# Decode attention: turning K in place on VectorE, and QK with a block-diagonal q

## The chip, the cores and the metric

One core of a Trainium2 chip. The metric is the device time of one execution in microseconds (us), lower is better. The experiments ran in five groups, each with the kernel before beside them and on another chip (0, 3, 14, 15 and 12 in the record); its medians agree within 0.2 us (384.60 to 384.79), so times are compared across groups. A ratio is the mean time of one kernel's fast runs over that of the kernel before in the same rounds, with a 95% interval, so it is not quite the ratio of the medians quoted beside it. The span in a profile is some 2 us shorter than the device time.

## The reference, cut to what matters

One decoding step of a transformer layer for a batch of 4: layer norm, attention over a sliding window of 4096 cached keys, and a gated MLP.

```python
B, Sq, D = 4, 1, 576
Hq, Hkv, Sk, Dh = 32, 16, 16384, 128
W = min(4096, max(256, Sk // 4))                       # 4096
q = (x @ wq) ...                                        # 32 heads of 128
k = jnp.repeat(k_cache[:, :, Sk - W:, :], rep, axis=1)  # rep = 2
v = jnp.repeat(v_cache[:, :, Sk - W:, :], rep, axis=1)
p = softmax(einsum("bhqd,bhkd->bhqk", q, k) * Dh ** -0.5)
o = einsum("bhqk,bhkd->bhqd", p, v) ... @ wo
h = x + attention(layernorm(x))
out = h + (relu(n @ W_gate) * (n @ W_up)) @ W_down      # n = layernorm(h)
```

K and V of the window are 67 MB each in bf16, the weights some 25 MB: 160 MB that have to come from HBM, for little arithmetic.

With these inputs the attention is only about 5e-5 in an output of about 0.05 (a float32 emulation off the chip gave standard deviations of 4.9e-5 and 0.049). **The comparison with the reference therefore hardly sees errors of the attention.**

## The kernel before

K and V each come in 16 tiles of 4 MB (one batch, four KV heads, all 4096 keys). A partition holds a block of 128 keys of one head: partition = 4 x (key block) + head. Four slots of SBUF form a ring, and all loads stand in one queue in program order: K0, wq (which takes one slot of the ring), K1, K2, K3, K4, V0, K5, V1, K6, V2 and so on. A load is issued when the last reader of its slot is done.

```python
def add_kv(kind, g):
    b, qd = divmod(g, 4)
    s = ring_slot()
    off = slot0 + s * TILE
    src = cache[b, 4*qd:4*qd+4, SK-WIN:SK, :].rearrange("a (p t) d -> p a (t d)", p=32)
    place((kind, g), off, TILE, ("TR", 4*g+3) if kind == "K" else ("PV", 4*g+3),   # who frees the slot
          lambda e: e.dma_start(out=arena[:, off:off+TILE], in_=src), key=f"slot{s}")
...
def pe_tr(i):            # TensorE turns K: 2048 transposes of 128x128 into PSUM
    ... e.transpose(out=bankb[TRB[j]][:, u*128:(u+1)*128], in_=kn[:, t, :], identity=perm)
def evac(i, j):          # VectorE and ScalarE take turns to bring it back to SBUF
    ... (dve e.tensor_copy | act e.copy)(out=kT[...], in_=bankb[TRB[j]])
def pe_qk(dd):           # q of one head against K, in four column groups side by side
    ... e.matmul(bank[4+w][32*j:32*j+32, :], lhsT=qTm[:, b, 4*qd+a, :], rhs=k[:, j, :, a, :], ...)
```

A K slot is free as soon as its transposes are done. The turned K lies in a buffer of its own, and q is needed only there.

## Time and profile before

384.78 us (median of 4, 384.63 to 384.81).

| engine | busy us | share |
|---|---|---|
| TensorE (PE) | 248.7 | 65% |
| VectorE (DVE) | 159.0 | 42% |
| ScalarE (ACT) | 146.4 | 38% |
| input DMA queue (q1) | | 97.4% of 16 engines |

From the profile's page of the kernel before: busy time by engine, two rows of the 40 slices (of 9.6 us each; digits are tenths), the DMA queues, the engines' shares of the chain that ended last, and the groups of instructions for turning K and for QK (busy us, mean ns of one, idle time before them).

```profile
PE 248.7 (65%) x3781; PEld 185.9 (49%) x3781; DVE 159.0 (42%) x277; ACT 146.4 (38%) x162; POOL 8.7 (2%) x36
DMA  8999999999999999999999999999999999999992
GB/s 329 439 433 432 410 421 437 434 433 433 425 423 433 427 433 435 427 420 433 437 430 435 424 428 427 427 428 439 437 432 415 421 436 451 416 431 426 416 411 113
...
q1 hardware_dynamic: 6352, 159.59, 97.4%
q8 instruction: 29, 0.48, 0.5%
...
DMA 69%; PE 27%; DVE 2%; SPq 1%; ACT 1%; issue 0%
...
L425 PE MATMUL psb<-sb_perm,sb_arena 128*128 128x128 bf16 x2048 | 140.3, 235 | 74.0 <-DMA sb_arena<-in_A_k_cache_dram 73.8
L441 ACT COPY sb_arena<-psb 128x1024 bf16<-128x1024 bf16 x128 | 123.0, 1021 | 141.1 <-PE psb L425 141.1
L439 DVE COPY sb_arena<-psb 128x1024 bf16<-128x1024 bf16 x128 | 87.0, 689 | 112.1 <-PE psb L425 111.6
L457 PE MATMUL psb<-sb_arena,sb_qTm 128*32 128x512 bf16 x512 | 38.0, 423 | 0.9 <-DVE sb_qTm L404 0.9
```

Read the GB/s row first: it never dips between the first slice and the last. The kernel is bound by its 160 MB at about 430 GB/s. Every engine has idle time and most of it (the last column) waits for DMA, or for an engine that does.

### The profile page before, as it was taken

Reading aid. Unit: us, or ns where it says so; the run is one execution under the profiler, and the core shown is the slowest. Engines: PE = TensorE matmul, PEld = TensorE weight load, DVE = VectorE, ACT = ScalarE, POOL = GpSimd, SP = SyncE. Lnnn points to the kernel's source line nnn. Section 1 sums busy time; section 2 is a strip of 40 time slices with the busy share of each in tenths; the row PEclk is TensorE's granted clock in tenths of the full one; section 3 lists DMA queues with packets and bytes.
Section 4 is the critical chain, followed back from the end, with each engine's and each line's share of the span. In section 5 each row is a group of like instructions: output and inputs, shape, how many; then the busy total and the mean of one; then the engine's idle time right before and its main releaser. Section 6 shows DMA issues by size and latency. Waiting matters only on the chain.

```text
span 382.6 us, 8170 instructions
## 1 busy us (share of the span) xinstructions
PE 248.7 (65%) x3781; PEld 185.9 (49%) x3781; DVE 159.0 (42%) x277; ACT 146.4 (38%) x162; POOL 8.7 (2%) x36
## 2 busy tenths in 40 slices
PE   0664999779492938893947667966759366026753
PEld 0643788557371726672726455745546222003532
DVE  3342565665342434774432426752516454002220
ACT  3341688836161524762433428542525401000010
POOL 7100000000000000000000000000000000000000
PEclk9997999999888796999796969996969657555597
DMA  8999999999999999999999999999999999999992
GB/s 329 439 433 432 410 421 437 434 433 433 425 423 433 427 433 435 427 420 433 437 430 435 424 428 427 427 428 439 437 432 415 421 436 451 416 431 426 416 411 113
DMA packets 6408, 160.09 MB, mean 418 GB/s; under 512 B 740, under 2 KB 744, under 8 KB 1384
## 3 DMA queue, kind: packets, MB, share of 16 engines
q1 hardware_dynamic: 6352, 159.59, 97.4%
q8 instruction: 29, 0.48, 0.5%
q14 instruction: 3, 0.02, 0.0%
q10 hardware_dynamic: 24, 0.01, 0.0%
HBM read 159.58 MB, written 0.00 MB: 417 GB/s over the span
## 4 chain that ended last, share of the span: by engine, by line
DMA 69%; PE 27%; DVE 2%; SPq 1%; ACT 1%; issue 0%
DMA sb_arena<-in_A_k_cache_dram 53%; PE psb L425 18%; DMA sb_arena<-in_B_W_down_dram 8%; DMA sb_arena<-in_A_v_cache_dram 8%; PE psb L457 5%; PE psb L505 2%; PE psb L480 1%; DVE sb_pp L487 1%; ACT sb_pp L468 1%; SPq L280 0%; DVE sb_stat L464 0%; DVE sb_o_sel L516 0%; PE psb L539 0%; PE psb L530 0%; DVE sb_o_tmp L512 0%
## 5 line engine op out<-in xcount | busy, mean ns | idle before, releaser
L425 PE MATMUL psb<-sb_perm,sb_arena 128*128 128x128 bf16 x2048 | 140.3, 235 | 74.0 <-DMA sb_arena<-in_A_k_cache_dram 73.8
L441 ACT COPY sb_arena<-psb 128x1024 bf16<-128x1024 bf16 x128 | 123.0, 1021 | 141.1 <-PE psb L425 141.1
L425 PEld LDWEIGHTS psb<-sb_perm,sb_arena 128*128 128x128 bf16 x2048 | 131.5, 106 | 89.3 <-DMA sb_arena<-in_A_k_cache_dram 79.8
L439 DVE COPY sb_arena<-psb 128x1024 bf16<-128x1024 bf16 x128 | 87.0, 689 | 112.1 <-PE psb L425 111.6
L505 PE MATMUL psb<-sb_arena,sb_pp 128*32 128x512 bf16 x512 | 35.9, 425 | 19.9 <-DMA sb_arena<-in_A_v_cache_dram 19.9
L457 PE MATMUL psb<-sb_arena,sb_qTm 128*32 128x512 bf16 x512 | 38.0, 423 | 0.9 <-DVE sb_qTm L404 0.9
L505 PEld LDWEIGHTS psb<-sb_arena,sb_pp 128*32 128x32 bf16 x512 | 12.9, 104 | 36.3 <-DMA sb_arena<-in_A_v_cache_dram 20.9
L512 DVE TENSOR_TENSOR sb_o_tmp<-psb,sb_qm 128x512 f32<-128x512 f32 x16 | 11.1, 692 | 41.2 <-PE psb L505 41.2
L487 DVE TENSOR_TENSOR sb_pp<-psb,sb_am 128x1024 bf16<-128x1024 bf16 x16 | 19.6, 1223 | 16.2 <-PE psb L480 16.2
L480 PE MATMUL psb<-sb_ident_b,sb_pp 128*128 128x128 bf16 x128 | 11.5, 242 | 15.8 <-DVE sb_pp L487 8.3
L468 ACT ACTIVATE sb_pp<-psb,sb_stat 128x2048 bf16<-128x2048 f32 x8 | 15.8, 1975 | 9.7 <-DVE sb_stat L466 9.7
L457 PEld LDWEIGHTS psb<-sb_arena,sb_qTm 128*32 128x32 bf16 x512 | 11.6, 103 | 14.8 <-issue 6.2
L480 PEld LDWEIGHTS psb<-sb_ident_b,sb_pp 128*128 128x128 bf16 x128 | 8.6, 108 | 18.8 <-ACT sb_pp L468 8.1
L516 DVE TENSOR_REDUCE sb_o_sel<-sb_o_tmp 128x128 f32<-128x512 f32 x16 | 16.4, 1024 | 0.5
L612 ACT COPY sb_pp<-psb 128x288 f32<-128x288 f32 x1 | 0.4, 399 | 36.2 <-PE psb L607 36.2
L654 PE MATMUL psb<-sb_arena,sb_hnT 128*32 128x384 bf16 x120 | 7.5, 421 | 4.1 <-DVE sb_hnT L639 2.2
L654 PEld LDWEIGHTS psb<-sb_arena,sb_hnT 128*32 128x32 bf16 x120 | 4.1, 121 | 7.2 <-DMA sb_arena<-in_B_W_up_dram 2.3
L464 DVE TENSOR_REDUCE sb_stat<-psb 128x1 f32<-128x1024 f32 x4 | 4.9, 1221 | 4.6 <-PE psb L457 4.6
L687 PE MATMUL psb<-sb_arena,sb_pp 128*32 128x144 bf16 x144 | 3.7, 251 | 4.1 <-DMA sb_arena<-in_B_W_down_dram 3.6
L534 ACT ACTIVATE sb_stat<-sb_stat 128x1 f32<-128x1 f32 x4 | 0.9, 213 | 13.1 <-DVE sb_stat L532 13.1
L661 DVE TENSOR_TENSOR sb_pp<-psb,sb_pp 128x384 bf16<-128x384 f32 x3 | 1.5, 551 | 9.6 <-PE psb L654 9.6
L687 PEld LDWEIGHTS psb<-sb_arena,sb_pp 128*32 128x32 bf16 x144 | 2.6, 105 | 5.1 <-DMA sb_arena<-in_B_W_down_dram 4.6
(128 smaller groups left out, 78.7 us busy)
## 6 DMA issues: line engine op xcount, KB each, us to landing
sb_arena<-in_A_k_cache_dram SPq DMA_DIRECT2D x16, 4096.0 KB, 28.3
sb_arena<-in_A_v_cache_dram SPq DMA_DIRECT2D x16, 4096.0 KB, 33.6
sb_arena<-in_A_wo_dram SPq DMA_DIRECT2D x1, 4608.0 KB, 20.7
sb_arena<-in_B_W_gate_dram SPq DMA_DIRECT2D x1, 4608.0 KB, 34.1
sb_arena<-in_B_W_up_dram SPq DMA_DIRECT2D x1, 4608.0 KB, 43.5
sb_arena<-in_A_wq_dram SPq DMA_DIRECT2D x1, 4096.0 KB, 23.0
sb_arena<-in_B_W_down_dram SPq DMA_DIRECT2D x3, 1296.0 KB, 30.0
sb_arena<-in_B_W_down_dram SPq DMA_DIRECT2D x1, 864.0 KB, 31.6
```

The source lines that it names most:

```text
L425: o = pe(("TRJ", i, j), lambda e, j=j, u=u, t=t: e.transpose(out=bankb[TRB[j]][:, u * 128:(u + 1) * 128], in_=kn[:, t, :], identity=perm[: ...
L439: dve(("EV", i, j), lambda e: e.tensor_copy(out=dst, in_=src), deps)
L441: act(("EV", i, j), lambda e: e.copy(out=dst, in_=src), deps)
L457: o = pe(("QK", dd), lambda e, a=a, j=j: e.matmul(bank[4 + w][32 * j:32 * j + 32, :], lhsT=qTm[:, b, 4 * qd + a, :], rhs=k[:, j, :, a, :], ...
L468: act(("EXP", b, w), lambda e: e.activation(out=p_sb[:, 2048 * w:2048 * w + 2048].rearrange("p (k a) -> p k a", a=4), in_=bass.AP(tensor=p ...
L480: pe(("PT", b, r), lambda e, tl=tl: e.transpose(out=mb_ps[:, tl * 128:(tl + 1) * 128], in_=p_sb[:, (r * 8 + tl) * 128:(r * 8 + tl + 1) * 128],
L487: dve(("PM", b, r), lambda e: e.tensor_tensor(out=dst, in0=src, in1=msk, op=ALU.mult), [("PT", b, r), "c_am8", ("PV", 16 * b - 1) if b els ...
L505: pe(("PV", i), lambda e, j=j, lo=lo, pm=pm, tb=tb: e.matmul(o_ps[32 * j:32 * j + 32, :], lhsT=pT[:, pm:pm + 32], rhs=v[:, lo:lo + 512], s ...
L512: dve(("OS", g), lambda e: e.tensor_tensor(out=o_tmp[:, :].rearrange("p (t d) -> p t d", t=4), in0=o_ps.rearrange("p (t d) -> p t d", t=4) ...
L516: dve(("OSEL", g), lambda e: e.tensor_reduce(out=o_sel[:, qd, :], in_=o_tmp[:, :].rearrange("p (t d) -> p d t", t=4), axis=AX.X, op=ALU.ad ...
L654: pe(("GU", g, c // 4), lambda e, g=g, m=m, j=j, lo=lo, c=c: e.matmul(bank[3 * g + m][32 * j:32 * j + 32, 0:384], lhsT=hnT[:, c if c < 4 e ...
L687: pe("DOWN", lambda e, j=j, r=r, n=n, wv=wv: e.matmul(bank[0][32 * n:32 * n + 32, 0:144], lhsT=hhT[:, r * 128 + 32 * j:r * 128 + 32 * j + 32],
```

## The change

Its intent: take the turning of K from TensorE, and the copies out of PSUM from VectorE and ScalarE. VectorE turns each half tile by one transpose of 128x4096 four-byte elements (pairs of bf16), in place; the layout takes it that this works in blocks of 32x32 (no trace shows the blocks). Since a pair of bf16 stays together, QK has to take the even and odd elements of d in separate matmuls; since the blocks are taken to stay in their 32 partitions, q is laid out block-diagonally over four groups of 32 partitions. The heads lie as partition mod 4, and the transpose writes them two by two: each 16 bytes of a partition of the turned K hold (head 0, key 0), (head 1, key 0), (head 0, key 1), (head 1, key 1), or the same of heads 2 and 3.

```diff
-            place((kind, g), off, TILE, ("TR", 4 * g + 3) if kind == "K" else ("PV", 4 * g + 3),
+            place((kind, g), off, TILE, ("QK", g, 1) if kind == "K" else ("PV", g),
...
-        def pe_tr(i): ... 2048 transposes on TensorE
-        def evac(i, j): ... 256 copies out of PSUM
+        def turn_k(g, w):
+            k = arena[:, land[("K", g)] + w * QWW:][:, 0:QWW].bitcast(FP32)
+            dst = k.rearrange("p (n h l a) -> p n l h a", h=2, l=2, a=2)
+            src = k.rearrange("p (n l h a) -> p n l h a", h=2, l=2, a=2)
+            dve(("TRA", g, w), lambda e: e.transpose(out=dst, in_=src), ...)
...
+        def pe_qk(g, w):
+            for a in range(4):            # head
+                for cb in range(4):       # half of d, even or odd
+                    off = land[("K", g)] + w * QWW + cb // 2 * 64 + a // 2 * 8 + a % 2 * 2 + cb % 2
+                    wo_ = b % 2 * QWW + (4 * qd + a) * 512 + cb * 128
+                    e.matmul(bank[SB[b % 2] + w], lhsT=arena[:, wo_:wo_ + 128],
+                        rhs=bass.AP(tensor=arena, offset=off, ap=[[AW, 128], [128, 64], [16, 4], [4, 2]]), ...)
```

(cuts marked with ...; P is turned on VectorE in the same way, its heads masked by the bias of the exponential; the tail is unchanged.) A K slot is now freed by QK, which needs q, and no longer by the transposes. And the pattern [4, 2] at the end of rhs says that a QK matmul finds exactly two elements in each 16 bytes of a partition, 8 bytes apart. (The texts call such 16 bytes a line.)

## The prediction

> **What bounds the kernel now.** DMA. The page gives 97.4% as the input queue's share of 16 engines, and every slice between the first and the last reads 9. In 4 us windows no stretch before 372 us is empty, whether PE is busy or idle (426 GB/s at 120-124 us with PE at zero). 160 MB over 2.5 to 379 us is 425 GB/s. In the chain of waits, 69% is DMA; its 18% of PE transposes are only what happened to be followed back through buffer releases while other transfers were queued. PE (65%), VectorE (42%) and ScalarE (38%) all have slack. So work taken from them is worth nothing unless it shortens the start (2.5 us) or the tail (3.3 us after the last landing), and neither is touched.
>
> **What the change removes.** 2048 PE transposes (140 us busy), their evictions on ScalarE (123 us) and VectorE (87 us), the P transposes (11.5) and masked copies (19.6).
>
> **What it adds.**
> - VectorE: 32 transposes of 4096 four-byte elements. The trace gives 1.04 ns per element (128x512 from PSUM 0.69 us, 128x1024 reduction 1.22), so about 4.4 us each, 8.8 a K tile, 140 in all. [...] Eight P transposes of 2048, 2.2 us each. VectorE ends near 210 us (55%).
> - PE: QK as 512 full-width matmuls of 512 columns instead of four side by side. Four took 0.245 us warm, 0.45 cold, so one should take 0.22 to 0.43: 7 to 10 us a tile, 115 to 150 us in all, against 178 for transposes plus QK before. [...]
> - ScalarE: 32 exponentials of 512 and 16 small q copies, near 30 us.
>
> **Critical path.** Steady state: one K and one V tile take 19.6 us of DMA. VectorE needs 8.8 + 1.7 (select) + about 1.6 (softmax share) = 12; PE 9 to 13. A K slot is freed about 15 us after landing (transpose 4.4, select 1.7, transpose 4.4, QK 3.5 to 5) instead of about 12; three other slots cover 29 us. No stall.
> Start: K slot 0 is now freed by QK, which needs q, not by the transposes. wq lands at 25-26 us; projection, q transposes and copies give q near 31-33 us; QK of tile 0 ends near 39-42. The queue still holds K2 until about 45 us, so K3 is issued with 1 to 4 us in hand. This is the tightest place; it could cost 0 to 3 us. The 8192-element memset on GpSimd (about 7 us from 0.84 ns per element) is ready near 10 us, before q.
> Tail: P of the last batch is ready about 27 us after K15 lands, as before (308 against 281 us), and after V15 all is as before.
>
> **Prediction.** 385.3 us, 8 in 10 between 382.5 and 391. Faster by over 2%: 0.02; within 2%: 0.87; slower: 0.11.
>
> **What would show it.** DMA tenths stay 9, GB/s near 425. VectorE transposes near 4.4 us and VectorE busy near 210. PE busy drops to 160-220, ScalarE below 50. Chain even more DMA. If the start step is wrong: a window below 300 GB/s at 38-50 us.
>
> **What would make it wrong.** If the four-byte transpose runs at half rate (8.7 us), VectorE needs about 20.5 us per pair, above DMA's 19.6: the last K is turned some 40 us late and the time rises 5% or more. If two-per-line reads slow QK twofold and the clock stays low, PE reaches 17 to 30 us a pair, similar. [...]

Three sentences are cut from it, where marked: two quoted rules, and one named a risk. The 4.4 us a transpose come from 1.04 ns per element and the 0.22 to 0.43 us a matmul from four side by side (0.245 and 0.45 us), both in the trace of the kernel before, and the forecast stays 385.3 us, 0.5 above the 384.78 before. That QK's read of two elements per 16 bytes costs nothing extra was the assumption; no trace had shown it.

## More of the kernel before

Times are of runs in the state that the record calls fast, unless a sentence says otherwise; for a kernel that was run once the state is unknown.

Keep the line "q8 instruction": 0.48 MB of instructions also go through the DMA engines.

The queue of SyncE (SP), which issues the loads, at the start of the kernel before (start us, duration, what):

```profile
2.51 24.92 SPq L239 DMA_DIRECT2D sb_arena<-in_A_k_cache_dram  x4
47.06 0.54 SPq L239 DMA_DIRECT2D sb_arena<-in_A_v_cache_dram  x1
56.37 0.53 SPq L239 DMA_DIRECT2D sb_arena<-in_A_k_cache_dram  x1
65.68 0.54 SPq L239 DMA_DIRECT2D sb_arena<-in_A_v_cache_dram  x1
```

The first line is K1 to K4: the last of them is issued by 27.4 us, long before the loads ahead of it have landed. One tile takes about 9.75 us of DMA (4.19 MB at about 430 GB/s), so there is always work queued.

## The result, and the profile after

400.09 us (median of 4, 399.88 to 400.25) against 384.78 before: ratio 1.0398 [1.0384, 1.0413], slower by 4.0%, outside the predicted range of 382.5 to 391. Executions over 1.5% slower than the fastest of the same kernel are left out of the means.

The same lines of the page, kernel after (slices of 10 us):

```profile
PE 297.6 (75%) x1629; PEld 94.5 (24%) x1629; DVE 209.3 (53%) x158; ACT 37.2 (9%) x94; POOL 16.2 (4%) x38
DMA  8999599978199999999999999999999999999994
GB/s 317 428 468 420 224 454 431 421 316 370 26 395 421 463 429 421 417 435 451 430 421 421 435 440 438 425 420 428 445 436 428 421 428 436 442 413 429 437 408 168
...
q1 hardware_dynamic: 6352, 159.59, 93.8%
q8 instruction: 12, 0.20, 0.2%
...
PE 53%; DMA 32%; DVE 13%; issue 1%; SPq 1%; ACT 0%
...
L439 PE MATMUL psb<-sb_arena 128*128 128x512 bf16 x512 | 223.1, 608 | 15.3 <-DVE sb_arena L422 13.2
L422 DVE STREAM_TRANSPOSE sb_arena<-sb_arena 128x4096 f32<-128x4096 f32 x32 | 141.5, 4435 | 50.5 <-DMA sb_arena<-in_A_k_cache_dram 50.5
```

The GB/s row now has holes at 40-50 and 80-110 us, and none later: all that is lost is lost in the first 112 us. In finer windows of the kernel after (4 us each: busy us of PE, PEld, DVE, ACT and POOL, then the granted clock, the DMA share and GB/s):

```profile
40.00:44.00 4.00, 4.00 (x11) 1.05 (x10) 2.70 (x1) 0.00 (x0) 0.00 (x0) 1.00 0.63 270
44.00:48.00 4.00, 4.00 (x10) 1.02 (x9) 2.80 (x1) 0.00 (x0) 0.00 (x0) 1.00 0.41 131
...
84.00:88.00 4.00, 2.71 (x7) 0.52 (x5) 1.23 (x1) 0.00 (x0) 0.00 (x0) 1.00 0.32 139
...
96.00:100.00 4.00, 4.00 (x10) 1.04 (x9) 4.00 (x2) 1.00 (x4) 0.00 (x0) 0.91 0.61 262
100.00:104.00 4.00, 4.00 (x11) 1.06 (x10) 4.00 (x3) 0.00 (x0) 0.00 (x0) 1.00 0.00 0
```

Against 425 GB/s, what these windows and their neighbours up to 112 us failed to move is worth 4.2 us (40-48), 2.7 (84-88), 0.6 (88-96) and 11.1 (96-112): 18.6 us. The span grew by 15.5. The 3 us between the two are the subject of the last experiments.

Why the DMA ran dry is in the chain of the kernel after (start us, duration, what):

```profile
31.30 55.43 PE psb L439 x128
86.73 0.02 issue
86.75 1.24 DVE sb_stat L446
...
89.63 4.37 DVE sb_arena L422
94.00 0.05 issue
94.05 13.97 PE psb L439 x32
108.02 1.87 PE psb L482 x32
```

and in the queue of SP of the same kernel:

```profile
2.51 43.98 SPq L240 DMA_DIRECT2D sb_arena<-in_A_k_cache_dram  x4
59.12 0.54 SPq L240 DMA_DIRECT2D sb_arena<-in_A_v_cache_dram  x1
72.93 0.54 SPq L240 DMA_DIRECT2D sb_arena<-in_A_k_cache_dram  x1
86.75 0.53 SPq L240 DMA_DIRECT2D sb_arena<-in_A_v_cache_dram  x1
108.05 0.54 SPq L240 DMA_DIRECT2D sb_arena<-in_A_k_cache_dram  x1
```

Each issue follows the end of one tile's QK. TensorE works without a break from 31.3 us, when q is ready, to 86.7: four K tiles in 55.43 us, 13.9 us each. The queue starts with five K tiles, and a tile arrives every 9.75 us. So each slot comes free some 4 us later than the one before it, counted against the DMA. Then the fifth tile's turn stands behind the softmax of batch 0 in VectorE's queue: the tile landed at 67.4 us, its turn starts at 89.6, and so its QK at 94.05 instead of 86.7. That QK takes another 13.97 us, and from about 99 us (the V tile issued at 86.75 is reported landed by the first DMA engine at 98.7 us, by the last at 100.8) to 108 us nothing is left to load. Later, K and V tiles alternate: 13.97 us of QK and 1.87 of PV are less than the pair's 19.5 us of DMA, and the loss does not grow.

The matmul is slow although the clock is full. Instructions of that line in the kernel after, 31 to 46 us (granted clock 1.00 in all its windows):

```profile
L439 PE MATMUL psb<-sb_arena x35: 607/609/617, 31.3 to 46.0; 128*128 128x512 bf16 x35
```

607 to 617 ns is the time from start to end of one matmul; successive ones overlap. What counts is how far apart they start, and the weight loads before them show it (start us, duration, what):

```profile
31.72 0.13 PEld L439 LDWEIGHTS psb<-sb_arena 128*128 128x128 bf16 x1 [0.29 <-issue]
32.15 0.13 PEld L439 LDWEIGHTS psb<-sb_arena 128*128 128x128 bf16 x1 [0.30 <-issue]
```

That is 0.43 us (55.43 us for 128 matmuls, 0.433 each). From 94.05 to 96.7 us, where the granted clock was 0.50, they start 0.43 us apart as well, and after it, at 1.00, still 0.43.

So the first theory: **a QK that finds two elements in each 16 bytes takes 0.43 us even at full clock, where four side by side of as many columns took 0.245 us in the kernel before, and the time is lost because five K tiles come in a row at the start.** Rivals: another property of rhs (its step, or the length of its contiguous run) or the full-width stationary slows the matmul; or the loss comes from slots being freed late whatever QK costs, or from VectorE's order, or from QK being slow in all 16 tiles.

### The profile page after: what moved, and what is told of

The parts are those of the page before. It is cut to its first block, busy times and chain, and to the rows that moved or that the text cites. A ratio compares the mean times of both kernels' runs of the same rounds, so it can differ in the third digit from the quotient of the medians.

```text
span 398.1 us, 3670 instructions
## 1 busy us (share of the span) xinstructions
PE 297.6 (75%) x1629; PEld 94.5 (24%) x1629; DVE 209.3 (53%) x158; ACT 37.2 (9%) x94; POOL 16.2 (4%) x38
## 4 chain that ended last, share of the span: by engine, by line
PE 53%; DMA 32%; DVE 13%; issue 1%; SPq 1%; ACT 0%
PE psb L439 45%; DMA sb_arena<-in_A_k_cache_dram 12%; DMA sb_arena<-in_B_W_down_dram 8%; DVE sb_arena L422 7%; DMA sb_arena<-in_A_v_cache_dram 6%; DMA sb_arena<-in_A_wq_dram 5%; PE psb L482 4%; DVE sb_o_sel L494 2%; DVE sb_stat L446 1%; PE psb L382 1%; DVE sb_o_tmp L490 1%; DVE sb_pp L469 1%; PE psb L519 0%; PE psb L454 0%; PE psb L448 0%
## 5 line engine op out<-in xcount | busy, mean ns | idle before, releaser
L439 PE MATMUL psb<-sb_arena 128*128 128x512 bf16 x512 | 223.1, 608 | 15.3 <-DVE sb_arena L422 13.2
L422 DVE STREAM_TRANSPOSE sb_arena<-sb_arena 128x4096 f32<-128x4096 f32 x32 | 141.5, 4435 | 50.5 <-DMA sb_arena<-in_A_k_cache_dram 50.5
L439 PEld LDWEIGHTS psb<-sb_arena 128*128 128x128 bf16 x512 | 57.7, 115 | 172.2 <-issue 153.3
L482 PE MATMUL psb<-sb_arena,sb_pp 128*32 128x512 bf16 x512 | 39.7, 467 | 21.0 <-DMA sb_arena<-in_A_v_cache_dram 16.1
L460 ACT ACTIVATE sb_pp<-psb,sb_stat 128x512 bf16<-128x512 f32 x32 | 25.0, 847 | 264.5 <-DVE sb_stat L455 264.5
L469 DVE STREAM_TRANSPOSE sb_pp<-sb_pp 128x2048 bf16<-128x2048 bf16 x8 | 17.9, 2271 | 0.0
L382 PE MATMUL psb<-sb_arena,sb_xnT 128*32 128x512 bf16 x32 | 3.6, 631 | 8.8 <-DMA sb_arena<-in_A_wq_dram 8.8
L298 POOL MEMSET sb_arena<- 128x8192 f32 x1 | 6.9, 6924 | 0.0
L460 ACT ACTIVATION_READ_ACCUMULATOR sb_pp<-psb,sb_stat 128x1 f32 x32 | 6.5, 202 | 0.0
L412 ACT COPY sb_arena<-sb_q_keep 32x128 bf16<-32x128 bf16 x16 | 4.9, 304 | 2.1 <-DVE sb_q_keep L404 1.9
## 6 DMA issues: line engine op xcount, KB each, us to landing
sb_arena<-in_A_wo_dram SPq DMA_DIRECT2D x1, 4608.0 KB, 14.8
```

Of the source, the lines that this page charges most:

```text
L298: pool("c_qW", lambda e: e.memset(arena[:, 0:2 * QWW].bitcast(FP32), 0.0))
L382: pe("QMM", lambda e, c=c, w=w, g=g, bk=bk: e.matmul(bank[4 + bk][32 * g:32 * g + 32, :], lhsT=xnT[:, c + bk if c == 4 else c, :], rhs=w, ...
L412: act(("QW", b), lambda e, i=i: e.copy(out=bass.AP(tensor=arena, offset=32 * i * AW + b % 2 * QWW + 32 * i, ap=[[AW, 32], [128, 4], [514, ...
L422: dve(("TRA", g, w), lambda e: e.transpose(out=dst, in_=src), [("L", "K", g)] if w == 0 else [])
L439: pe(("QK", g, w), lambda e, off=off, wo_=wo_, qd=qd, first=first, last=a == cb == 3: e.matmul(bank[SB[b % 2] + w], lhsT=arena[:, wo_:wo_ ...
L460: act(("EXP", b, w), lambda e, w=w, a=a: e.activation(out=bass.AP(tensor=pp, offset=4096 + a // 2 * 2048 + w * 1024 + a % 2, ap=[[8192, 12 ...
```

## The experiments

### What slows QK

e1 reads four elements per 16 bytes, e2 a contiguous run of 512, e3 two adjacent elements in each 16 bytes, e4 one per 16 bytes. Only K's read pattern, with its offset, differs (in e1 the transpose and P's order as well). e2, e3 and e4 give wrong scores; the comparison with the reference reported all three correct, which shows how little it sees.

```diff
 # the change                      ap=[[AW,128],[128,64],[16,4],[4,2]]   two per 16 bytes, 8 bytes apart
+# e1_four_per_line                ap=[[AW,128],[128,64],[2,8]]          plain transpose(out=k, in_=k)
+# e2_rhs_contiguous               ap=[[AW,128],[1,512]]
+# e3_rhs_adjacent                 ap=[[AW,128],[128,64],[16,4],[1,2]]
+# e4_rhs_one_per_line             ap=[[AW,128],[128,64],[8,8]]
```

> Correct result wanted. K is turned without the swap inside each 32-byte group; each QK matmul takes eight adjacent bf16 pairs, so its moving operand has four elements per 16-byte line (4 bytes apart) instead of two (8 bytes apart); P is written contiguously and turned from there. Theory A (the moving operand's read decides: a line with two hits gives half rate): QK starts 0.216 us apart when the clock is full, against 0.432 now; QK of tile 0 ends near 39 us, K3 is issued near 39 instead of 45.9 us, and the kernel returns to 384 to 387 us. Theory B (a full-width matmul of 512 columns with 128 weight columns takes 0.43 us here whatever it reads): spacing stays 0.43 and the time stays 400. Theory C (even four per line is not enough, only dense reads are): spacing stays 0.43, but the contiguous run below falls to 0.216.

> Wrong result on purpose: the changed kernel, with QK's moving operand 512 adjacent bf16 of the same half tile; all else as is. Theory A: spacing 0.216 us at full clock, time 384 to 387 us. Theory B: 0.43 us and 400 us.

> Wrong result on purpose: two elements per 16-byte line as in the change, in the same lines, but adjacent (2 bytes apart) instead of 8 bytes apart. Theory A1 (hits per line count): 0.43 us, 400 us. Theory A2 (the step between neighbours counts, more than 4 bytes is slow): between 0.216 and 0.43, as half of the steps are short; time below 397 us.

> Wrong result on purpose: one element per 16-byte line (16 bytes apart). Theory A1: one line per column costs twice as much as in the change, 0.86 us apart; QK alone is then 27.6 us a tile, above the 19.6 us that DMA needs for a pair, so the kernel takes at least 540 us. If a line that is used once costs the same as one used twice (rate limited per column, not per line), spacing stays 0.43 and the time 400 us. Theory B: 0.43 us.

The group of QK matmuls in each of e1, e3 and e4 (page, part 5; in e1 the line is L437), and for e1 16 matmuls in a row (start us, duration):

```profile
L437 PE MATMUL psb<-sb_arena 128*128 128x512 bf16 x512 | 139.9, 436 | 54.3 <-DVE sb_arena L420 52.2
...
133.32 3.63 PE L437 MATMUL psb<-sb_arena 128*128 128x512 bf16 x16 [0.50 <-DVE sb_arena L420]
```

```profile
L439 PE MATMUL psb<-sb_arena 128*128 128x512 bf16 x512 | 223.1, 608 | 15.0 <-DVE sb_arena L422 12.8
```

```profile
L439 PE MATMUL psb<-sb_arena 128*128 128x512 bf16 x512 | 441.5, 1035 | 6.7 <-DVE sb_arena L422 4.6
```

| elements per 16 bytes | 16-byte pieces per matmul | us apart | ns per piece | time, us | ratio |
|---|---|---|---|---|---|
| 8 (e2) | 64 | 0.216 | 3.38 | 381.71 (2 runs) | 0.9921 [0.9901, 0.9941] |
| 4 (e1) | 128 | 0.216 | 1.69 | 381.69 | 0.9931 [0.9914, 0.9947] |
| 2, adjacent (e3) | 256 | 0.431 | 1.68 | 400.07 (one run, state unknown) | - |
| 2, 8 bytes apart (change) | 256 | 0.432 | 1.69 | 400.09 | 1.0398 |
| 1 (e4) | 512 | 0.862 | 1.68 | 622.97 (one run, state unknown) | - |

The spacings of e1 to e3 are medians between the starts of successive weight loads in the trace, at the granted clock of 1.00. Below four elements per 16 bytes the spacing goes with the number of pieces: one and two elements in each both cost 1.7 ns a piece. (Pieces of another size do not fit: the change and e4 both touch 256 pieces of 32 bytes, at 0.432 and 0.862 us; the change touches 512 pieces of 8 bytes and most matmuls of e3 256, at 0.432 and 0.431.) The step within the 16 bytes does not matter (e3 equals the change to 0.1 us of busy time), nor does the full-width stationary (e1 has it too, at 0.216 us). Four per piece give 0.216 us for 512 columns, the shortest spacing measured, and more (e2) gains nothing. This holds at the full clock alone: in the windows of e9, which also reads four per 16 bytes, 20 matmuls fall in 4 us where the granted clock was 1.00 (84 to 88 us) and 11 where it was 0.50 (100 to 104 us); the change, two per 16 bytes, has 11 at 1.00 (100 to 104 us), and starts them 0.43 us apart at 0.50 too, as said above. So at 0.50 the two-per-16-bytes read costs nothing extra that these runs show. (The first matmuls of e1, at 31.7 to 35.5 us, are 0.427 us apart as well, although the mean granted clock up to 48 us reads 1.00; this is not explained.) With four per 16 bytes the kernel is not only rid of the loss but 0.7% faster than before.

**e1 is not a solution.** It was meant to be correct, and the comparison reported it correct, but an emulation off the chip with inputs scaled so that attention matters showed that its groups of four mix the heads (the code shows it too: partition = 4 x key block + head, so after a plain transpose the four neighbours in 16 bytes are heads 0 to 3). Its time counts, its values do not.

### Which part of the loss comes from where

e6 gives batch 0 alone e2's contiguous read, e7 the other three batches; both are wrong. e8 is the change with both turns of tile 4 put ahead of batch 0's softmax in VectorE's queue; it is correct.

```diff
+# e6: ap = [[AW,128],[1,512]] if b == 0 else the change's     e7: the other way round
 # e8:
...  (the two turns of tile 4 are left out of their usual place)
+            if g == 3:
+                turn_k(4, 0)
+                turn_k(4, 1)
             if qd == 3:
                 softmax(b)
```

> Wrong result on purpose: QK reads 512 adjacent elements in batch 0 alone (K tiles 0 to 3), two per line as in the change in the other three batches. If the loss is made in the start, where five K tiles arrive one after the other at 9.8 us each while PE needs 13.9 us for each, and later K and V alternate (19.6 us a pair, PE about 16): 382 to 387 us. If half-rate QK costs everywhere alike: about 396 us.

> Wrong result on purpose, the reverse of e6: two per line in batch 0, 512 adjacent elements in the other three. Start theory: 392 to 400 us, most of the loss stays. Alike everywhere: about 388 us.

> The change with one order altered: the two transposes of K tile 4 stand before batch 0's softmax on VectorE, which in the change holds them back until QK of tile 3 is done (PE idle 86.8 to 94.0 us but for two small matmuls). QK of tile 4 should start near 89.5 instead of 94.05 us, and as the chain there is PE without a gap, the whole kernel should gain 4 to 5 us: 395 to 396.5 us. If the loss were not a chain through PE at that place, nothing is gained: 400 us.

The GB/s row of e6, and QK of tile 4 in e8 (start us, duration):

```profile
GB/s 332 442 404 423 431 428 417 430 442 435 442 426 411 436 438 437 431 424 419 438 438 435 430 424 428 436 435 435 428 419 435 435 438 427 416 445 425 430 404 180
...
89.34 13.97 PE L439 MATMUL psb<-sb_arena 128*128 128x512 bf16 x32
```

e6 (two runs of each of the three): 382.26 us, ratio 0.9937 [0.9917, 0.9957], all of the loss gone, though 12 of 16 tiles still read two per 16 bytes. e7: 394.78 us, ratio 1.026; it recovers 5.3 us, which fits the fast QK of tile 4, the first of batch 1 (this share was not separated). e8: 395.71 us, ratio 1.029: QK of tile 4 starts at 89.34 instead of 94.05 us and 4.4 us are won. So the slow QK costs nothing in the steady state, and the start is where the 15 us go. The order on VectorE is a part of it, about 4 us. The gains of e6, e7 and e8 (17.8, 5.3 and 4.4 us) overlap and are not to be added.

### A correct kernel without the loss: three tries

**e5_scatter** writes on VectorE so that four keys of one head share 16 bytes; QK then reads four per 16 bytes. The transpose then writes one element per 16 bytes.

```diff
-            dst = k.rearrange("p (n h l a) -> p n l h a", h=2, l=2, a=2)
+            dst = k.rearrange("p (n h l) -> p n l h", h=4, l=4)
...  (src likewise; rhs of QK ends in [32, 2], [2, 4])
```

> The right way to four per line (e1 turned out to mix the heads: its time counts, its result doesn't; the comparison with the reference can't see that, since attention is a small part of the output). Here VectorE writes each turned block so that four blocks of keys of one head stand in one 16-byte line; QK then reads four per line and all else is as in the change. VectorE's own writes now go to another line with every element. If VectorE pays for that as TensorE's reads do, its transposes grow from 4.4 to 7 us or more, K takes 14 us or more of VectorE a tile, and the start loses time again (390 to 410 us). [...] QK spacing 0.216 us at full clock either way.

(The sentence cut from it put the rival in terms of a rate that no run shows. Its outcome was: transposes stay at 4.4 us, and the kernel takes 381 to 383 us.)

408.98 us (406.12 to 411.67), ratio 1.0655 [1.0607, 1.0704]. From its page:

```profile
L422 DVE STREAM_TRANSPOSE sb_arena<-sb_arena 128x4096 f32<-128x4096 f32 x32 | 235.9, 7420 | 2.1 <-DMA sb_arena<-in_A_k_cache_dram 2.1
L439 PE MATMUL psb<-sb_arena 128*128 128x512 bf16 x512 | 143.2, 441 | 77.4 <-DVE sb_arena L422 75.4
```

QK is fast (143 us), but the transpose went from 4.44 to 7.42 us, 1.81 ns per element instead of 1.08: two of them, 14.8 us a tile, again exceed the tile's 9.75. The cost moved from TensorE's read to VectorE's write. For VectorE's write two of its four-byte elements per 16 bytes are as fast as four (4.44 us in the change and in e1), for TensorE's read two of its two-byte elements are not (0.432 us against 0.216).

**e9_two_dma** leaves VectorE's pairs and loads K by two DMAs per tile, to the even and to the odd partitions, so that neighbouring partitions hold the same head. (I found no way to write it as one DMA; no run shows that there is none.)

```diff
+                two = win.rearrange("a (u s t) d -> s u a (t d)", u=16, s=2)
+                half = lambda i: lambda e: e.dma_start(out=arena[i:128:2, off:off + TILE], in_=two[i])
...  (half(0) and half(1) are issued one after the other; turn_k and rhs follow the new order)
```

> The change with a layout that gives QK four elements of one head per 16-byte line and is meant to be correct: each K tile comes by two DMAs, one to the even and one to the odd partitions, so that partition 8u + 2 head + s holds key block 2u + s; the in-place turn on VectorE writes two elements (s = 0, 1) per line as before. My theory (QK was slow because only two of the four-byte-strided elements it reads lie in each line, and that stall is lost in the start): QK near 140-150 us in all, a matmul every 0.216 us, transposes at 4.4 us as in the change, 381 to 383 us like the two fast runs before, ratio near 0.993. Rival (a DMA to 64 of 128 partitions, every second one, moves slower than one to all 128): the rate falls below 425 GB/s in K tiles, time above 388 us although QK is fast.

606.3 us (median of the four fast runs, 604.58 to 611.84; two more, 614.42 and 636.9, were slow), ratio of the fast runs 1.578: the rival's mechanism, far larger than its number. Two lines of the page:

```profile
GB/s 208 312 258 218 217 208 210 326 227 316 236 306 243 302 249 296 249 275 264 272 264 217 275 225 274 217 282 209 219 230 234 264 374 134 286 247 434 429 422 137
L445 PE MATMUL psb<-sb_arena 128*128 128x512 bf16 x512 | 151.3, 464 | 158.3 <-DVE sb_arena L428 156.2
```

A 32 KB packet takes 1.21 us in the kernel before; in e9 most take 2.3 to 2.6 us, and 1.21 while wq loads (24 to 32 us); in e11, whose batch 1 loads K by one DMA again, they take 1.21 us from 96 to 168 us. The DMA engines are just as busy (every slice from the first to the 33rd reads 9) and move half. That this pair of DMAs, each to every second partition, is slow is shown; why it moves half is open.

**e13_pair_batch0** changes no load and no transpose. Only batch 0 is in the critical start, and in batch 0 two more PSUM banks are free. So there a matmul takes all four elements of 16 bytes, two keys of each of two heads, with the q of both heads in its block-diagonal stationary. The scores fill four banks instead of two; the columns of the wrong head are never used, since each exponential takes every second column.

```diff
+                    if b == 0:
+                        h, th = divmod(a, 2)
+                        off = land[("K", g)] + w * QWW + th * 4096 + cb // 2 * 64 + h * 8 + cb % 2
+                        wo_ = (2 * qd + h) * 512 + cb * 128
+                        rhs, dst, first = [[AW, 128], [128, 32], [16, 4], [2, 4]], 2 * w + th, h == cb == 0
...
-                        in_=bank[SB[b % 2] + w], func=ACT.Exp,
+                        in_=bank[SB[b % 2] + w] if b else bass.AP(tensor=psb, offset=1024 * w + a % 2, ap=[[4096, 128], [2, 512]]), func=ACT.Exp,
 # q of batch 0 is put in pairs of heads; its block is zeroed again on GpSimd before batch 2; batch 0's maximum runs over four banks
```

> The change, correct, with a QK for batch 0 alone that reads all four elements of a 16-byte line: the line holds two keys of each of two heads, so one matmul scores both heads (q of both in the stationary block), the scores take four PSUM banks instead of two (they are free in batch 0), and the exponentials take every second column. Batches 1 to 3 as in the change, two per line. No load differs from the change. Theory (only the stall at the start is lost, because five K tiles arrive there in a row at 9.75 us each while a slow QK needs 13.97): as e6_fast_batch0, 382 to 383 us, the matmuls of batch 0 at 0.22 us, no window below 350 GB/s before 370 us. Rival (the slow QK of the other 12 tiles costs as well, or the pair's wider maximum and strided exponentials bring a wait): above 386 us.

382.51 us (382.23 to 383.63, 5 runs), ratio 0.9951 [0.9938, 0.9963]: 17.6 us better than the change and 0.5% better than the kernel before, by an interval that excludes 1. From its page, and the first line of SP's queue:

```profile
GB/s 331 441 407 419 434 438 438 436 421 421 438 422 414 435 441 423 407 438 439 438 434 431 426 424 438 436 424 438 427 426 438 434 427 415 407 461 413 436 402 193
...
L448 PE MATMUL psb<-sb_arena 128*128 128x512 bf16 x512 | 200.6, 561 | 18.7 <-DVE sb_arena L425 16.7
```

```profile
2.51 39.28 SPq L240 DMA_DIRECT2D sb_arena<-in_A_k_cache_dram  x4
```

K1 to K4 are issued by 41.8 us instead of 46.5, there is no hole in the row, and TensorE is still busy 273.7 us, 24 less than in the change. That is the claim in a correct kernel: with the slow QK kept in 12 of 16 tiles, nothing is lost.

### Is it correct? Two checks on the chip

Since the comparison hardly sees attention, e15 lets batch 1 of e13 take batch 0's K and q through the change's own path, and adds to the output the largest squared difference of the two paths' scores, times 1e4 and summed over partitions. e16 does the same with the two head pairs of each 16 bytes exchanged in batch 0. e11 and e12 did it for e9's layout.

```diff
+dve(f"chkd{a}", lambda e, s0=s0: e.tensor_tensor(out=s0, in0=psb[:, 4:6, :] ..., in1=s0, op=ALU.subtract), ...)
+# e16 only: off = ... + (1 - h) * 8 ...
```

> Not for time. e13 with batch 1 taking batch 0's K and q through the change's two-per-line path; the largest squared difference of the scores of the two paths, times 1e4 and summed over partitions, is added to the output. Same scores: reported correct, error below 0.001. Different scores (they have a standard deviation of 0.03): wrong by thousands.

> Not for time. The same with the two head pairs of a line exchanged in the QK of batch 0: must be reported wrong, by some 25000 (emulated off the chip). If it is reported correct, the check on the chip is blind.

> Not for time. Batch 1 takes batch 0's K and q but goes through the change's own load, turn and QK; the largest squared difference between its scores and those of batch 0 through the two-DMA layout, times 1e4 and summed over partitions, is added to the output. If both layouts give the same scores, the result is reported correct (maximum error below 0.001). If they differ, scores of standard deviation 0.03 make the output wrong by thousands. Batch 1's attention is wrong on purpose, which lies below the tolerance of the comparison.

> Not for time. The same with even and odd partitions of the two-DMA load exchanged, which mixes up the keys' order: the scores differ and the output must be reported wrong, by thousands (the emulation off the chip gave 22144). If it is reported correct, the on-chip check is blind as well.

e15 and e11 were reported correct, e16 and e12 wrong (relative errors of 508688 and 448995). So the scores of e13 are those of the change, and the check can see a mistake. That the change's own scores are right, and the scores' way on to the output (exponentials, PV), were checked only by an emulation off the chip with scaled inputs, where e13's largest error was 0.0037, as that of the change.

### Why e13 is 2 us faster than the kernel before

e1, e2, e6 and e13 all end 2 to 3 us below the kernel before, with the same bytes to load. One candidate was the instructions themselves: 3672 instead of 8170, 0.20 MB instead of 0.48 MB of instruction fetch through the DMA engines. The test adds 4500 one-element memsets on idle GpSimd of which nothing depends.

```diff
+        for n in range(4500):
+            pool(None, lambda e, n=n: e.memset(junk[:, n:n + 1], 0.0))
```

> The same kernel with 4500 one-element memsets on idle GpSimd, of which nothing depends. Theory that the kernels with fewer instructions are about 3 us faster than the kernel before because less instruction fetch goes through the DMA engines and the slowest engine lags less at the end: more packets of instruction fetch (0.2 to near 0.5 MB), the last landings spread from about 3.4 us to 6 us over the engines, time 1 to 3 us longer than without the memsets. Rival (the 3 us come from elsewhere, for instance an earlier order of loads): the time stays within 0.5 us of the run without memsets.

> e13 with 4500 one-element memsets on idle GpSimd, of which nothing depends. Theory that kernels with fewer instructions are 2 to 3 us faster than the kernel before because less instruction fetch goes through the DMA engines and the slowest engine lags less at the end: 0.3 MB more instruction fetch, a wider spread of the last landings (3.2 to about 6 us), time 1 to 3 us longer than e13. Rival: time within 0.5 us of e13.

Both failed as tests. e10 (612.57 us over its five fast runs, ratio 1.595, against e9's 1.578) drowns in e9's half-rate loads and says nothing. e14 (440.04 us): the memsets stood ahead of the zeroing of batch 2's q block in GpSimd's queue, and the first copy of that q waited 129.5 us. e17 puts them behind it, and e18 halves them.

> e14 mended: the 4500 memsets stand behind the last work of GpSimd that anything waits for (the zeroing of batch 2's q block at about 60 us). Theory (instruction fetch on the DMA engines is what the fewer instructions save): 0.3 MB more instruction fetch in 8 KB packets of 0.31 us, 11 us of one DMA engine's time if one carries them all, less if several share them; last landings spread wider than e13's 2.1 us, time 0.5 to 3 us longer than e13's 382.5. Rival (the 2 us of e13 against before come from elsewhere): within 0.4 us of e13.

> Half as many memsets. Theory: half the extra time of e17 or less. Rival: no order between e13, e18 and e17.

e18: 391.57 us, ratio 1.018 [1.016, 1.020]. e17: 402.98 us, ratio 1.048 [1.046, 1.049]. So 9.1 us for 18 more packets of instruction fetch, 20.5 us for 36: 0.5 to 0.6 us each. The order that the theory asked for came, but 20.5 us stand against the 0.5 to 3 that I had expected. From the page of e17:

```profile
GB/s 314 463 421 419 414 434 447 420 422 435 442 411 419 443 429 408 403 292 442 274 415 445 439 355 429 271 369 424 307 422 421 434 447 301 437 436 411 463 396 164
q14 instruction: 38, 0.31, 0.2%
L428 DVE STREAM_TRANSPOSE sb_arena<-sb_arena 128x4096 f32<-128x4096 f32 x32 | 141.6, 4436 | 76.9 <-DMA sb_arena<-in_A_k_cache_dram 76.9
```

The transpose takes the same 4.44 us as ever, so GpSimd's memsets do not slow it; VectorE waits for loads (76.9 us, against 48.8 in e13). A load is split over 16 DMA engines, each of which reports its share in the trace. The time in us from the first engine's report to the last one's, for loads landing near:

```
landing at   before   e13    e18    e17
  45 us        1.9     1.8    1.8    1.5
 105 us        2.0     1.4    3.7    5.6
 162 us        3.5     1.7   10.5   12.5
 183 us        3.5     1.8   11.8   14.7
 240 us        5.0     1.7    5.3   13.2
 the last      6.6     2.1    2.1    3.4
```

In e17 at 185 us the last engine is 12.6 us behind the last but one: all of GpSimd's fetches (38 packets, nearly all of 8 KB) fall on one engine, which still has its share of every load. A load has landed only when the slowest engine is done (in e1 the turn of K2 starts at 45.11 us, with the last engine's report at 45.1, not with the first at 43.3), so that one engine holds all up, until slots come free late and the other 15 run dry: the dips of the row.

In the kernel before the lag grows in steps of about 1.5 us (2.0, 3.5, 5.0, 6.5), as if the 16 KB fetches of q8 (29, of 1.07 us each in the median) fell on several engines in turn. Its last load lands on its first engine at 372.8 us and on its last at 379.4; in e13 at 375.1 and 377.2. The end is set by the slowest engine, which in e13 is 2.2 us earlier, and the spans differ by 2.3 us. In e1 the first engine lands at 372.9 us, as in the kernel before, and the last at 376.4, 3.0 us earlier; its whole gain is in the lag. The mechanism is shown by e17 and e18 for GpSimd's instructions. That the 17 packets more of the queue q8 (29 against 12; the instructions that went are nearly all TensorE's) cost the kernel before these 2.2 us is inferred from the steps; no run changed TensorE's instructions alone.

## Why the prediction was wrong, point by point

- **The step that failed: QK's read of two elements per 16 bytes was taken to cost nothing extra.** e1 to e4 show 1.7 ns per 16-byte piece for TensorE's moving operand below four elements in each, so with two a matmul takes 0.432 us, against 0.216 with four. The prediction's "0.22 to 0.43" per matmul held the true 0.43 only as that of a low clock, and it reckoned 7 to 10 us a tile: 13.97 were measured, and 223 us in all instead of 115 to 150. So PE's busy time rose to 297.6 us instead of falling to 160 to 220, and the DMA's share of the chain fell from 69% to 32%.
- **The start, "0 to 3 us", was mis-sized for that reason, and for a second one.** It was the right place, it was named as the tightest, and the window below 300 GB/s at 38 to 50 us came as announced. But the estimate looked at the first slot only. Five K tiles come in a row, so the 4 us by which each is too slow add up. And the order on VectorE (tile 4's turn behind the softmax) was not costed: e8 puts 4.4 us to it. The DMA windows lost 18.6 us, not 0 to 3.
- **"Steady state ... No stall" was right in its conclusion**, with 15.8 us of PE a pair in place of the 9 to 13 reckoned, because the DMA's 19.5 left room: e6 and e13 keep the slow QK in 12 tiles and lose nothing.
- **"If two-per-line reads slow QK twofold and the clock stays low, PE reaches 17 to 30 us a pair"** named the cause among its risks, but in the wrong place: the pair costs 15.8 us, under the DMA's 19.5, and the harm is done before there are pairs.
- **VectorE was right**: 4.435 us a transpose (4.4 predicted) and 209 us in all (210). The trace of the kernel before had given 1.04 ns per element of a partition, from other operations; the transposes took 1.08, with two and with four elements per 16 bytes on the write side, but e5 shows 1.81 with one.
- **q at 31.3 us (31 to 33), GpSimd's memset of 6.9 us (7), ScalarE at 37 us (below 50): right.** The tail was right to 1.5 us (41.9 us from V15's landing to the end, 40.4 before); P was ready 31 us after K15 landed, not 27, and the GB/s row shows no dip for it.
- **"DMA bounds it, so work taken from the engines is worth nothing": nearly right.** It missed that in a kernel with 4500 fewer instructions the slowest DMA engine lands some 2 us earlier (that the instructions are the reason is inferred, as said above).

## What to carry to other kernels

Count the 16-byte pieces that a matmul's moving operand touches, not its elements alone: here four elements in each took 0.216 us a matmul, two 0.432, one 0.862. Pack four elements of use into each, by widening the stationary if the data cannot be moved. Where DMA is the bound, do not compare an engine's work with the steady state alone; find the stretch in which the loads come in the order that is hardest for it, and add up its deficit over the whole row of tiles. And check correctness with something that can fail: an output to which attention adds a thousandth tells nothing about the attention.
